# Row tiles of a group transposed and measured during two products instead of four, and two closing sums one product later

## The chip, the core and the metric

The kernel runs on one core of a Trainium2 chip. Its engines are TensorE (PE in the profile; PEld is its weight loads), VectorE (DVE), ScalarE (ACT), GpSimd (POOL) and SyncE (SP), which only issues DMAs here. Each engine works through its own instructions in order, and semaphores tie the engines together. The metric is the time of one execution in microseconds on the device, the median of several runs; less is better.

## The reference

Inputs are q, k, v of shape (8, 8, 576, 64), a threshold `tau`, and two matrices of 512 x 2048 and 2048 x 512. All is fp32.

```
scores = 0.125 * q @ k^T                       # per batch and head, 576 x 576
scores = where(scores >= max(row) - tau, scores, -1e9)
attn   = softmax(scores) @ v                   # (8, 8, 576, 64)
x      = attn with heads side by side          # (8, 576, 512)
u      = x + real(fft over 512 of fft over 576 of x)
un     = (u - mean(u)) / sqrt(var(u) + 1e-6)   # over the 512 columns
out    = u + relu(un @ w_ch1) @ w_ch2
```

## The kernel before, in words

**Three kinds of work are interleaved by hand.** The order of the program is the order of each engine's queue; nothing is reordered later.

*Attention.* For each batch there are four pairs of heads, and for each pair five row tiles of queries (four of 128 rows, and a short one made of the two heads' last 64). One pass of the main loop handles one row tile `i`: `scores` (L440, L446) puts the scores of two heads into PSUM; `softmax_first` takes row maxima on VectorE (L520) and exponentials on ScalarE (L526); `softmax_second` applies the threshold and sums on VectorE (L540, L385, L388); `softmax_third` scales on ScalarE (L549). The row tile before it is meanwhile transposed on TensorE (L587, L605: tiles `pe` and `pw`) and copied out by ScalarE (L593, L607). Twice per pair the product with v follows (L636).

*Mixing.* When a batch's attention is done, the two Fourier transforms are products with cosine and sine tables (`mixing`, L743: `py` at L766, `pa` at L783 and L787). Their PSUM tiles are copied out by ScalarE (L771, L776, L799) or summed by VectorE (L803, L804). The result, `u` transposed (`u_t`), has channels in the partitions and tokens along the free dimension. Sums over folded inputs (`fold_rows` L669 with L687 and L692, `partial_sums` L725, and L751 to L756) prepare it. `settle` (L459) lets a mixing overwrite `u_t` only when the groups before have read their rows.

*The two products with the big matrices.* Tokens are handled in nine groups of 512. The first group uses plain products (`channels`, L904). The other eight use `two_level` (L1107), which replaces ordinary block products with Winograd's seven-product form, applied twice. First comes the product with the first matrix: 28 quanta of matmuls (L1210). Then the product with the second matrix: seven **products** `m` in the order `L1 = (1, 2, 5, 4, 6, 7, 3)`, numbered `at = 0..6`, each of seven **quanta** `jn = 0..6` of four matmuls (L1398). Quanta 0 to 3 of a product fill one PSUM bank `po`, quanta 4 to 6 a second one. After quantum 3 and after quantum 6 the bank is copied out by ScalarE (L1410) or added to a running sum by VectorE (L1412, L1418). Jobs on other engines hang at certain quanta in the table `side` (`at_slots(at, slots, jobs)`): combinations of operands for the next product (`l2_forms`, L1191; `l1_form`, L1168), `gather` (L1274 to L1278, run by `plus`, L1263), and `finish`, which adds a finished quarter, times 1/std, to the rows (`Rows.add`: reciprocal L890 once per group, then L895).

The last group (`whole`, g = 8) has another form for its last products and another table of jobs.

**Row tiles.** The result needs `u` with tokens in the partitions. `Rows.load(t)` (L854) transposes the `t`-th 128 tokens: four transposes on TensorE into one PSUM tile `pn` (L858), then four copies by ScalarE into the tile `u` (L863, L864). It also leaves a job in `measures`: mean and variance on VectorE (`bn_stats` L869, `bn_aggr` L870). The main loop runs the waiting jobs with `measure()` right after `softmax_second`. When a group's four rows are loaded, `two_level` appends it to `wanted`; the main loop, after `softmax_third`, then calls `factors()` (L879): pending statistics first, then on ScalarE a square root (L881) and an exponential that brings back the exponential's table (L884), each with a table load. `finish` does the same itself where the main loop hasn't yet. In the first and in the last stretch of the kernel, statistics follow at once on the load.

**What sets the order.** In each pass the main loop calls `fill` three times: `fill(True)` between `softmax_first` and `softmax_second`, one between the two halves of the transposed weights, one after `softmax_third`. Each gets a budget of matmul columns (`per_slot`, about 3,900) and draws quanta (2048 columns each) from the group in work until it is spent; a row tile counts 512 columns, in a step of its own. While mixing goes on, a step of it is drawn first. Jobs hung at quanta within `fill(True)` are held back until after `softmax_second` and the statistics.

**Buffers.** All of `pe`, `pw`, `pv`, `pn`, `py`, `pa`, `ph` and `po` share four PSUM banks (tag "mm", `bufs=4`); the scores take the other four. The rows' tiles `u` have four buffers. The weights' blocks come from DRAM in loads of four quanta each into three buffers (`ensure`, L1068), issued two loads ahead.

The places that the change touches are the job table (L1341) and the end of each quantum (L1419 to L1426) in `two_level`:

Of the kernel before, what the change touches and what calls it, by code (L numbers as in the profile page):

```python
# [47 lines left out]
def kernel(  # L48
# [1038 lines left out]
    def block(g, second, index):  # L1087

        n = len(LOADS) * (g - 1) + (7 if second else 0) + index // PER
        if index % PER == 0:  # L1090
            ensure(n + 2 if g > 1 or second or index < 20 else n + 1)
        return w1[n % 3][:, 512 * (index % PER) : 512 * (index % PER + 1)]

    def quadrant(k, i):
# [7 lines left out]
    v_u, v_11, v_22, v_21, v_12 = (  # L1102
        w2_all[:, 3072 + NV * n : 3072 + NV * (n + 1)] for n in range(5)
    )
    v_22_21 = w2_all[:, 3072 + 2 * NV : 3072 + 4 * NV]

    def two_level(g, rows):  # L1107
# [157 lines left out]
        def twice(x):  # L1265
            return bass.AP(
                tensor=x.tensor, offset=x.offset, ap=[list(x.ap[0]), [0, 2], list(x.ap[-1])]
            )

        def gather(eng, v):  # L1270

            v = v.rearrange("p (j n) -> p j n", n=128)
            return [
                plus(eng, v[:, 1:5:3], twice(v[:, 0])),  # L1274
                plus(eng, v[:, 5], v[:, 4]),
                plus(eng, v[:, 6], v[:, 2]),
                plus(eng, v[:, 6], v[:, 4]),
                plus(eng, v[:, 2:4], twice(v[:, 5])),  # L1278
            ]
# [19 lines left out]
        def finish(i, n, v):  # L1299
            if wanted:  # L1300
                wanted.pop().factors()
            v = v.rearrange("p (j n) -> p j n", n=128)
            cols = slice(256 * n, 256 * n + 256)
            second = v[:, 3]
            second = bass.AP(
                tensor=second.tensor, offset=second.offset,
                ap=[list(second.ap[0]), [-128, 2], [1, 128]],
            )
            return [
                lambda: rows.add(2 * i, cols, v[:, 1:7:5]),  # L1310
                lambda: rows.add(2 * i + 1, cols, second),
            ]
# [8 lines left out]
        def at_slots(at, slots, jobs):  # L1321
            for jn, job in zip(slots, jobs, strict=True):
                side.setdefault((at, jn), []).append(job)

        whole = g == NG - 1
# [12 lines left out]
        at_slots(3, (0,), l1_form(s1_tile, s1_tile, a11, (V, V, V, V))[3:4])  # L1338
        at_slots(4, (1, 2, 4, 6), l1_form(a12, a12, s1_tile, (P, P, P, P)))
        at_slots(2, (0, 1, 2, 3, 4), gather(P, v_11))  # L1340
        at_slots(4, (2, 4), [lambda n=n: finish(0, 0, v_11)[n]() for n in range(2)])  # L1341
        if not whole:
            at_slots(
                5, (0,), [lambda: P.tensor_tensor(out=v_12, in0=v_u, in1=v_22, op=ALU.add)]
# [15 lines left out]
        def slot(at, jn):  # L1360
            while held:
                held.pop(0)()
            held.extend(side.get((at, jn), ()))
            while held and not holding:
                held.pop(0)()

        def plain_product(at, m):

            x = a[m].rearrange("p (k s i n) -> p k i s n", k=2, i=2, n=128)
            banks = plain[m] = [  # L1370
                ps.tile([128, 512], FP32, tag="mm", bufs=4, name="po")[:, 0:256] for _ in range(2)
            ]
            for jn, (n, k, at_) in enumerate(((0, 0, 0), (0, 1, 1), (1, 1, 2), (1, 0, 3))):
                right_ = plain_block(m, at_)
                for i in range(2):
                    for s in range(4):
                        nc.tensor.matmul(  # L1377
                            banks[i][:, 128 * n : 128 * n + 128], x[:, k, i][:, s],
                            right_[:, 128 * s : 128 * (s + 1)],
                            start=jn == 0 and s == 0, stop=jn % 2 == 1 and s == 3,  # L1380
                            skip_group_check=True,
                        )
                slot(at, jn)
                if at < 6 or jn < 3:
                    yield 4096

        for at, m in enumerate(L1):
            if whole and at > 4:
                yield from plain_product(at, m)
                continue  # L1390
            for jn, j in enumerate(J):
                if jn in (0, 4):
                    bank = ps.tile([128, 512], FP32, tag="mm", bufs=4, name="po")
                c0 = 128 * (jn % 4)
                to = bank[:, c0 : c0 + 128]
                right_ = block(g, True, 7 * at + jn)
                for s in range(4):
                    nc.tensor.matmul(  # L1398
                        to, lefts[m][j][:, s], right_[:, 128 * s : 128 * (s + 1)],
                        start=jn in (0, 4) and s == 0, stop=s == 3, skip_group_check=True,  # L1400
                    )
                if jn in (3, 6):
                    first, end = (0, 512) if jn == 3 else (512, NV)
                    src = bank[:, 0 : end - first]

                    def here(v):
                        return v[:, first:end]

                    if m in (1, 5, 4):
                        nc.scalar.copy(here({1: v_u, 5: v_22, 4: v_21}[m]), src)  # L1410
                    elif m == 2:
                        V.tensor_tensor(out=here(v_11), in0=here(v_u), in1=src, op=ALU.add)  # L1412
                    elif m == 6 and whole:
                        to = v_22_21.rearrange("p (two n) -> p two n", two=2)[:, :, first:end]
                        V.tensor_tensor(out=to, in0=to, in1=twice(src), op=ALU.add)
                    else:
                        to = here(v_12 if m == 3 else v_u)
                        V.tensor_tensor(out=to, in0=to, in1=src, op=ALU.add)  # L1418
                slot(at, jn)  # L1419
                if jn == 3 and at < 4:  # L1420
                    rows.load((2, 3, 0, 1)[at])
                    if at == 3:
                        wanted.append(rows)
                    yield ND * 128
                if jn < 6:
                    yield 2048  # L1426
            background()
            if m != 3:
                yield 2048
# [39 lines left out]
    def background():  # L1469

        if late:
            fold_more()
# [157 lines left out]
    def start_batch(b):  # L1630

        nonlocal groups, todo, per_slot, budget
        mixes.append(mixing(b))
        todo += MIX
        while groups < NG and BT * (groups + 1) <= (b + 1) * S:
            rows = Rows(groups)
            work.append((b, channels(rows) if groups == 0 else two_level(groups, rows), rows))
            todo += cost(groups)
            groups += 1

        keep = 4 * BT * (NJ - 2) * DM // 128 if b == 0 else 3 * 7 * 2048
        per_slot = (todo - spent - keep) / (3 * per_batch)
        budget = spent
# [103 lines left out]
    for i in range(2 * per_batch, total):  # L1747


        n, t = divmod(i, NT)  # L1750
# [157 lines left out]
```

## Time and profile before

| what | value |
|---|---|
| median of 3 runs | 1552.85 us (1552.24 to 1553.26) |
| the profiled execution | 1552.55 us |
| its span, first to last instruction | 1550.8 us |
| granted TensorE clock, mean | 0.999 |
| row tile's transposes (L858) | 144, 273 ns each by the profile |
| row tile's copies (L863, L864) | 72 and 72, 283 and 293 ns |
| statistics (L869, L870) | 36 and 36, 682 and 182 ns |
| closing sums of quarters (L895, 256 columns) | 64, 622 ns |
| table loads (L881, L884) | 9 and 9, 1283 ns |

The second-level products of groups 1 to 8 start at 441.0, 607.3, 778.1, 949.0, 1118.1, 1287.5, 1405.1 and 1499.7 us. In each of these groups the row tiles are now loaded after quantum 3 of products 0, 1, 2 and 3; in group 4 at 954.6, 966.3, 975.0 and 987.8 us. From about 1327 us on no attention is left, and the rest of the products and of the mixing runs alone.

How to read it: times are in microseconds unless marked ns. Matmul ends are modelled, and matmuls overlap, so the duration of a matmul says less than the distance between starts. In a row of the timeline, the first number is the start from the beginning of the span, the second the duration, and the bracket at the end the idle time of that engine just before, with what ended it. In a row of waits, "A <- B" means that A sat idle until B was done.

### The profile page before, as it was taken

How to read it: one execution, taken by the hardware profiler on the slowest of the kernel's cores; microseconds unless marked ns; L12 is line 12 of the kernel's file. 1: busy time of each engine (PE TensorE's matmuls, PEld its weight loads, DVE VectorE, ACT ScalarE, POOL GpSimd, SP SyncE). 2: the span in 40 equal slices, each digit the busy share in tenths (PEclk: the TensorE clock that was granted, in tenths of full speed). 3: DMA queues.
4: the chain of work that ended last, by engine and by line, in shares of the span. 5: the costliest groups of instructions: out<-in, count | busy, mean ns of one | idle time of the engine just before them, and what ended most of it. 6: DMA issues, size and time to landing. Idle time of an engine off the chain costs nothing.

```text
span 1550.8 us, 27036 instructions
## 1 busy us (share of the span) xinstructions
PE 1523.1 (98%) x9786; PEld 1185.1 (76%) x9786; DVE 1066.9 (69%) x2141; ACT 917.1 (59%) x1921; POOL 776.8 (50%) x964
## 2 busy tenths in 40 slices
PE   8999999999999999999999999999999999999999
PEld 5555555556788777877788778887788778989999
DVE  7987676846779466866588566956687666746546
ACT  6875675655656576656766666666666676232131
POOL 3775553034365643545254724555264626646635
PEclk9999999999999999999999999999999999999999
DMA  6423233465866344634464354635464534646655
GB/s 168 132 59 119 78 92 108 136 204 159 269 200 189 111 150 133 195 102 141 143 186 140 117 159 135 195 93 166 125 191 135 159 117 140 221 163 226 236 198 184
DMA packets 248907, 239.31 MB, mean 154 GB/s; under 512 B 197027, under 2 KB 218533, under 8 KB 228678
## 3 DMA queue, kind: packets, MB, share of 16 engines
q1 hardware_dynamic: 246262, 237.28, 50.1%
q8 instruction: 78, 1.28, 0.3%
q10 hardware_dynamic: 2512, 0.30, 0.1%
q14 instruction: 55, 0.45, 0.1%
HBM read 205.93 MB, written 31.46 MB: 153 GB/s over the span
## 4 chain that ended last, share of the span: by engine, by line
PE 84%; DVE 9%; ACT 3%; DMA 1%; POOL 1%; issue 1%; SPq 0%; ACTq 0%; DVEq 0%; POOLq 0%
PE ph L1210 25%; PE po L1398 18%; PE sc L440 9%; PE pv L636 9%; PE pw L605 7%; PE po L933 4%; PE ph L909 2%; PE sc L446 2%; PE py L766 2%; PE pa L783 1%; PE pe L587 1%; PE pa L787 1%; PE pm L360 1%; PE po L1377 1%; PE pn L858 1%
## 5 line engine op out<-in xcount | busy, mean ns | idle before, releaser
L520 DVE TENSOR_REDUCE neg<-sc 128x1 f32<-128x576 f32 x216 | 154.2, 750 | 113.0 <-PE sc L440 99.6
L526 ACT ACTIVATE e<-sc,neg 128x576 f32<-128x576 f32 x216 | 158.6, 734 | 121.6 <-DVE neg L520 121.5
L1147 DVE TENSOR_TENSOR hs<-ph,hs 128x512 f32<-128x512 f32 (+1 forms) x128 | 105.4, 823 | 168.0 <-PE ph L1210 97.7
L1398 PE MATMUL po<-w,w_all 128*128 128x128 f32 x1728 | 219.4, 276 | 0.3 <-ACT ends L593 0.3
L1398 PEld LDWEIGHTS po<-w,w_all 128*128 128x128 f32 x1728 | 205.0, 192 | 9.4 <-issue 4.0
L1156 POOL TENSOR_TENSOR w<-hs 128x512 f32<-128x512 f32 x32 | 42.1, 1317 | 313.8 <-ACT hs L1152 240.0
L540 DVE SCALAR_TENSOR_TENSOR e<-sc,thr,e 128x576 f32<-128x576 f32 x216 | 168.3, 812 | 20.6 <-ACT thr L530 20.6
L1210 PE MATMUL ph<-u_t,w 128*128 128x256 f32 x768 | 180.9, 382 | 0.5 <-DMA w<-f 0.5
L440 PE MATMUL sc<-kT,qT 64*128 64x288 f32 x1024 | 169.8, 431 | 7.1 <-DVE e L477 6.1
L607 ACT COPY e_t<-pw 128x512 f32<-128x512 f32 x256 | 148.6, 595 | 44.1 <-PE pw L605 42.7
L605 PE MATMUL pw<-ident,e 128*128 128x128 f32 x1152 | 168.8, 273 | 6.0 <-ACT ends L593 1.9
L549 ACT ACTIVATE e<-e,den 128x576 f32<-128x576 f32 x216 | 157.4, 775 | 8.9 <-DVE den L388 8.2
L1210 PEld LDWEIGHTS ph<-u_t,w 128*128 128x128 f32 x768 | 140.9, 190 | 23.6 <-issue 5.3
L1210 PE MATMUL ph<-w_all,w 128*128 128x256 f32 x672 | 157.1, 382 | 1.1 <-DVE w_all L1132 1.0
L605 PEld LDWEIGHTS pw<-ident,e 128*128 128x128 f32 x1152 | 134.8, 141 | 21.9 <-issue 5.6
L1152 ACT ACTIVATE hs<-hs 128x512 f32<-128x512 f32 (+1 forms) x96 | 74.1, 772 | 114.5 <-DVE hs L1147 113.7
L1210 PEld LDWEIGHTS ph<-w_all,w 128*128 128x128 f32 x672 | 123.4, 190 | 23.9 <-issue 4.9
L440 PEld LDWEIGHTS sc<-kT,qT 64*128 64x128 f32 x1024 | 96.3, 187 | 57.1 <-issue 23.7
L1263 POOL TENSOR_TENSOR w_all<-w_all 128x128 f32<-128x128 f32 (+2 forms) x160 | 118.4, 757 | 29.1 <-DVE w_all L1418 20.2
L1398 PE MATMUL po<-w,hs 128*128 128x128 f32 x912 | 120.0, 278 | 0.3 <-ACT ends L593 0.3
L1398 PEld LDWEIGHTS po<-w,hs 128*128 128x128 f32 x912 | 109.9, 192 | 9.9 <-issue 8.0
L593 ACT COPY ends<-pe 128x128 f32<-128x128 f32 (+1 forms) x128 | 38.1, 298 | 58.7 <-PE pe L587 40.1
(227 smaller groups left out, 2945.3 us busy)
## 6 DMA issues: line engine op xcount, KB each, us to landing
w<-f SPq DMA_DIRECT2D x150, 1024.0 KB, 4.9
hs<-in_moe_w_ch_dram SPq DMA_DIRECT2D x23, 512.0 KB, 4.7
q_in<-in_q_dram SPq DMA_DIRECT2D x128, 72.0 KB, 4.3
out_dram<-u SPq DMA_DIRECT2D x36, 256.0 KB, 2.5
k_in<-in_k_dram SPq DMA_DIRECT2D x124, 72.0 KB, 2.4
v_in<-in_v_dram SPq DMA_DIRECT2D x64, 128.0 KB, 5.0
f<-w SPq DMA_DIRECT2D x14, 512.0 KB, 3.3
f<-w SPq DMA_DIRECT2D x7, 1024.0 KB, 4.8
```

The costliest lines, as they stand in the source:

```text
L440: nc.tensor.matmul(sc[j][:, c, 0:HALF], qT[hp, 128 * t : 128 * t + 128], kT[hp, k0 + HALF * c : k0 + HALF * (c + 1)], start=True, stop=True,)
L520: nc.vector.tensor_reduce(out=neg[:, j : j + 1], in_=sc[j][:, :, 0:HALF], axis=AXIS_XY, op=ALU.max, negate=True,)
L526: nc.scalar.activation(out=ej, in_=sc[j][:, :, 0:HALF], func=ACT.Exp, bias=neg[:, j : j + 1], scale=1.0)
L540: nc.vector.scalar_tensor_tensor(out=ej, in0=sc[j][:, :, 0:HALF], scalar=thr[:, j : j + 1], in1=ej, op0=ALU.is_ge, op1=ALU.mult, accum_out ...
L549: nc.scalar.activation(out=e[:, S * j : S * (j + 1)], in_=e[:, S * j : S * (j + 1)], func=ACT.Copy, scale=den[:, j : j + 1],)
L605: nc.tensor.transpose(pw[:, c, :], e[:, c0 : c0 + 128], ident[:, :])
L607: nc.scalar.copy(e_t[:, 4 * j : 4 * j + 4, qs], pw[:, :, :])
L636: nc.tensor.matmul(pv[64 * j : 64 * j + 64, 0:m], vt[:, 2 * c + j, :], e_t[:, 4 * j + c, 0:m] if c < 4 else ends[:, 0, 0:m], start=(c == 0 ...
L1147: nc.vector.tensor_tensor(out=to, in0=bank, in1=to if other is None else other, op=ALU.add)
L1210: nc.tensor.matmul(bank[:, 256 * q : 256 * q + 256].rearrange("p (two n) -> p two n", two=2), left[:, 256 * c + 128 * q : 256 * c + 128 * ...
L1263: return lambda: eng.tensor_tensor(out=to, in0=to, in1=other, op=ALU.add)
L1398: nc.tensor.matmul(to, lefts[m][j][:, s], right_[:, 128 * s : 128 * (s + 1)], start=jn in (0, 4) and s == 0, stop=s == 3, skip_group_check ...
```

## The change

In `two_level`, row tiles are loaded after quanta 3 and 6 of products 0 and 1 (before: after quantum 3 of products 0 to 3), in the same order 2, 3, 0, 1. The group is appended to `wanted` with the last of them, after product 1's last quantum. In all groups but the last, the two closing sums of the first quarter (`finish(0, 0, v_11)`: rows 0 and 1, columns 0 to 255) hang at quanta 2 and 4 of product 5 instead of product 4. In the last group they stay where they are.

```diff
         at_slots(2, (0, 1, 2, 3, 4), gather(P, v_11))
-        at_slots(4, (2, 4), [lambda n=n: finish(0, 0, v_11)[n]() for n in range(2)])
+        at_slots(
+            4 if whole else 5, (2, 4), [lambda n=n: finish(0, 0, v_11)[n]() for n in range(2)]
+        )
...
                 slot(at, jn)
-                if jn == 3 and at < 4:
-                    rows.load((2, 3, 0, 1)[at])
-                    if at == 3:
+                if jn in (3, 6) and at < 2:
+                    rows.load((2, 3, 0, 1)[2 * at + jn // 6])
+                    if (at, jn) == (1, 6):
                         wanted.append(rows)
                     yield ND * 128
                 if jn < 6:
```

## The prediction

> **What bounds the kernel now.** I read the page's first part, then the time by stages, then the waits of TensorE, then single stretches of the timeline. The totals:
>
> ```profile
> PE 1523.1 (98%) x9786; PEld 1185.1 (76%) x9786; DVE 1066.9 (69%) x2141; ACT 917.1 (59%) x1921; POOL 776.8 (50%) x964
> ```
>
> TensorE is busy for 98%, and everything else has gaps. Here a rule has to be weighed. The Trainium skill (page "Perfetto Trace Analysis", section "Identifying the Most-Contended Engine") says that matmul busy time is no measure of headroom, since matmuls are pipelined, and that the weight loads' busy share is. By it 24% of the span, 366 us, would be open. So I took neither figure, but the time from the start of one block of matmuls to the start of the next, less what the same pair of blocks usually takes. That leaves 53 us in the whole span, 29 of them in the first 440 us, ahead of any second-level product, and 24 after it, of which 12 come in crumbs of up to 0.15 us. The change moves no matmul off TensorE. Its effect can be only in these stalls, and in new ones.
>
> The waits of TensorE name the stalls inside the second-level products:
>
> ```profile
> PE py L766 <- ACT y_e L776: 2.4, 5, 0.7
> PE pw L605 <- ACT ends L593: 1.9, 1, 1.9
> PE pw L605 <- ACT w_all L1410: 1.5, 1, 1.5
> PE pw L605 <- DVE w_all L1418: 1.1, 1, 1.1
> PEld po L1398 <- ACT ends L593: 1.0, 2, 0.5
> ```
>
> (Waiter, releaser, us in total, times, longest. The 1.9 is before 300 us, out of the change's reach.) All are one kind: the four "mm" banks of PSUM are taken, and TensorE waits until an eviction on ScalarE or VectorE frees one. The first row recurs in the fifth to sixth product of the groups. In group 4 (products from 949.0 to 1037.5 us) the timeline shows how it arises:
>
> ```profile
> 1000.95 0.17 DVE L388 RECIPROCAL den<-den 128x2 f32<-128x2 f32 x1
> 1001.03 0.16 DVE L890 RECIPROCAL rstd<-rstd 128x4 f32<-128x4 f32 x1
> 1001.22 0.95 DVE L895 SCALAR_TENSOR_TENSOR u<-w_all,rstd,u 128x256 f32<-128x256 f32 x1
> ...
> 1004.36 0.48 DVE L895 SCALAR_TENSOR_TENSOR u<-w_all,rstd,u 128x256 f32<-128x256 f32 x1
> ...
> 1005.22 1.42 DVE L520 TENSOR_REDUCE neg<-sc 128x1 f32<-128x576 f32 x2
> ...
> 1006.06 0.74 ACT L526 ACTIVATE e<-sc,neg 128x576 f32<-128x576 f32 x1 [1.28 <-DVE neg L520]
> ...
> 1008.19 0.52 PEld L766 LDWEIGHTS py<-dim_s,f 128*128 128x128 f32 x4 [0.91 <-ACT y_e L776]
> ```
>
> (Start, us, engine, line; in brackets idle time and what ended it.) The scores were ready at 1002.0, but VectorE reached their maxima only at 1005.22, because it runs in order and had the closing sums (L890, L895) and the mixing sums ahead of them. The exponentials wait for the maxima, the eviction of the first py waits behind the exponentials on ScalarE, and TensorE waits for that bank. The same chain stands in groups 3 and 5.
>
> **The change part by part.**
>
> 1. *Closing sums of the first quarter (L895, with L890) from product 4 to product 5 (counted from 0).* In seven groups two sums and one reciprocal leave the place shown: 0.16 + 0.95 + 0.48 = 1.6 us less on VectorE ahead of those maxima. TensorE there lacks 0.83 us by the start-to-start count (0.91 idle in the weight loads less the usual 0.08). 1.6 covers it, so it goes: groups 3, 4, 5 at 839.0, 1008.2, 1177.6, together **2.5 us**. Group 1 has 0.35 at 497.4 of the same kind. Group 2 has 1.22 at 666.0, where pw waits for L1418, which stands behind the same sums (1.1 us there). Together **1.6 us**. In the new place one sum and the reciprocal (0.6 us) stand in front of the next iteration's maxima; VectorE comes there 1.6 us earlier than now, so these are no later. The other falls into a held stretch, behind the softmax, where VectorE idles 3.1 us before L1418 at 1018.7. Cover gone, each would cost at most its own 0.6 us. What is late next: only the store of rows 0 and 1, which still waits for the second half's sums.
>
> 2. *Statistics and factors earlier.* Per group the same four L869 + L870 (0.68 + 0.18 us), so nothing is added, but two leave the stretch from product 2 to 3. In group 4 the one at 989.34 runs straight before 5 us of folding (L687, L692) that also delay the maxima:
>
> ```profile
> 989.34 0.69 DVE L869 BATCH_NORM_STATS2 stats<-u 128x6 f32<-128x512 f32 x1
> 990.07 0.18 DVE L870 BATCH_NORM_AGGREGATE mv<-stats 128x2 f32<-128x6 f32 x1
> 990.17 1.79 DVE L687 TENSOR_TENSOR half<-x 128x287 f32<-128x287 f32 x2
> ```
>
> That gives part 1 another 0.9 us of margin. The factors (two table loads, square root, warming exponential) move from about 993 to about 975 us in group 4. In group 2 they ran from 651.5 to 654.6, and the 0.46 us stall at 656.6 (eviction of pe on ScalarE) stands right behind: **0.5 us** off.
>
> 3. *Transposes and evictions earlier.* Each row tile is four transposes (0.45 us of TensorE) and four copies (L863, L864: 0.8 us of ScalarE together), as many as before. In group 3 the third tile sat between two product banks and pw waited for the fifth bank (1.52 us idle, 1.68 by starts, at 808.6); with that tile gone four banks suffice: **1.7 us** off. Against it: a tile counts 512 columns in the fills, so the products' quanta slip by at most one from the end of product 0 to the middle of product 3, and are back after it. By that count all middle groups come to what group 3 has now: the last quantum of product 2's first bank and the first of its second are issued just after the scores, and product 3's first bank has to wait for an eviction that stands behind the exponentials. TensorE reaches it some 12.45 us after the scores of the short row tile (967.67 in group 4). VectorE, with two statistics in that iteration instead of one, starts the next maxima at about +9.95 instead of 976.78 - 967.67 = +9.1; two exponentials with the threshold take until +12.3, the eviction (L1410, 0.59) until +12.85. That is **0.4 us lost** in each of groups 2 to 5, **1.6 us**; from below 0, from above 1.3 (L1191 took 1.57 us there and takes 0.68 elsewhere). Elsewhere there is room: in product 1 VectorE idles 1.6 us before the maxima at 968.84, and the second tile of a product meets banks freed 0.5 us or more before.
>
> The factors in the new place are the second weighing. Rows: 1.28 + 0.30 + 1.28 + 0.20 = 3.1 us in a row:
>
> ```profile
> 651.51 1.28 ACT L881 ACT_TABLE_LOAD   x1
> 652.80 0.30 ACT L881 ACTIVATE rstd<-mv,eps 128x4 f32<-128x4 f32 x1
> 653.11 1.28 ACT L884 ACT_TABLE_LOAD   x1
> 654.40 0.20 ACT L884 ACTIVATE warm<-eps 128x1 f32<-128x1 f32 x1
> 654.51 0.46 ACT L1410 COPY w_all<-po 128x384 f32<-128x384 f32 x1
> ```
>
> The Trainium skill (page "ScalarE: Activation LUTs", section "What ACT_TABLE_LOAD costs") says the same 1283 ns for a load but 2.66 us for every switch with its drain, 5.3 us for two, and that speaks against the change. Begun at 975.2, 3.1 us end at 978.3, before the maxima let the exponential start at 978.4: free. 5.3 us end at 980.5, 2.1 us later, and the stall in front of product 3 becomes 2.5 us in four groups, 10 us. The copy at 654.51 starts straight behind the last activation, so I take the row's 3.1.
>
> 4. *No queue is passed.* Loading a row tile and its statistics issue no DMA. The weights' loads on SyncE (w<-f, 4.9 us to land, issued two loads of four quanta ahead) slip with their quanta by at most one, some 0.9 us; q, k and v queued behind them are wanted iterations later. GpSimd's gather of v_11 stays in product 2, so the sums wait for it less than now. The tail (groups 7 and 8) has TensorE dense, with no stall between 1450 and 1547 us; fewer statistics there buy nothing.
>
> **The sum.** Off: 2.5 + 1.6 + 0.5 + 1.7 = 6.3 us. On: 1.6, plus 0.8 that I put for bank waits which a new order of evictions makes (the trace has four such singles of 0.4 to 1.7 in eight groups). Net -3.9 us, on the profiled execution's 1552.55 (span 1550.8 and 1.75 around it): 1548.65. The median of the runs is 0.3 higher, so **1549.0 us**.
>
> **The rivals.**
>
> *The stalls are only moved (within 0.2%).* For it: TensorE's whole loss in the products is 6.3 us, and with banks this scarce a wait removed at one place is met at the next: if half of the gain is met again, 1552.85 - 3.1 + 2.4 = 1552.1 us. Against it: 839, 1008 and 1178 repeat to 0.01 us, so one cause is at work, and it is the one taken away.
>
> *Slower: product 3's first bank.* The mechanism of part 3, in the iteration after the short row tile: factors, two statistics and the exponentials ahead of one eviction. It decides when the loss in each of the four groups is over (6.3 + 3.1) / 4 = 2.35 us; with the page's table cost it is 2.5, and with 0.8 us for the rest the time is 1552.85 - 6.3 + 10 + 0.8 = 1557.4 us. For it: VectorE has no gap over 0.4 us between 971 and 983 us. Against it: the 3.1 us row.
>
> *The loads free the mixing, which may not begin to overwrite before a group's rows are read.* They don't: in group 4 the last tile is read at 987.8, and the mixing first asks at 1020.9, 33 us later. This alone would be no change, 1552.85.
>
> **How the numbers follow.** 0.2% of the time is 3.1 us, about what this kernel's measurement can tell from no change. Forecast case 0.50 (its own range 1546.4 to 1549.7, all faster); stalls moved 0.32 and mixing 0.03, both within; slower by the bank 0.15. So faster 0.50, same 0.35, slower 0.15. The range 1546.2 to 1554.8 leaves out some 0.05 below and most of the slower case above.
>
> **What would show it.** Right: no wait of py on L776 of 0.7 us in groups 3 to 5; pairs of L858 blocks at quanta 3 and 6 of products 0 and 1; maxima in the iteration of the first py at about 1 us after their scores instead of 3.2; L881 some 18 us earlier in a group. Wrong: TensorE waiting at the first quantum of product 3 for L1410 by over 1 us, a table block over 3.1 us long, or pw waiting for u's copies (L864).

## The result and the profile after

| | median of the runs | profiled execution | its span |
|---|---|---|---|
| before | 1553.05 us (1552.24 to 1553.77, 4 runs) | 1552.55 us | 1550.8 us |
| after | 1545.76 us (1543.60 to 1547.94, 4 runs) | 1547.94 us | 1546.2 us |

The ratio is 0.996, with a 95% interval of 0.9947 to 0.9973: faster by 0.3 to 0.5%. 1549.0 us was forecast, with a range from 1546.2 to 1554.8: the direction is right and the size too small. The median lies just below the range; the ratio, applied to the 1552.85 us that the forecast started from, gives 1546.6, just inside. In the kernel after, lines behind the job table are two higher: L1398 is L1400, L1410 is L1412, L1418 is L1420.

The first part of the page of the kernel after:

```profile
PE 1524.0 (99%) x9786; PEld 1186.0 (77%) x9786; DVE 1063.2 (69%) x2141; ACT 916.4 (59%) x1921; POOL 779.4 (50%) x964
```

No engine has fewer instructions. What shrank is the span between the same 9786 matmuls, 4.6 us in this pair of executions. The waits of TensorE (PE) in the kernel after show where (us in total, times, longest):

```profile
PE pw L605 <- ACT ends L593: 1.9, 1, 1.9
...
PE py L766 <- ACT y_e L776: 0.9, 5, 0.2
...
PE pw L605 <- DVE w_all L1420: 0.2, 1, 0.2
```

The 1.9 is the wait before 300 us that was out of reach. Of the others, py waits 0.9 us in five places instead of 2.4, the wait for L1418 (now L1420) fell from 1.1 to 0.2, and the rows of pw for L1410 (1.5) and of po for L593 (1.0 in the row of the weight loads) are gone. No row is new.

In group 4 the iteration of the first py read so before (the timeline, cut; the maxima followed at 1005.22):

```profile
1000.65 1.36 PE L440 MATMUL sc<-kT,qT 64*128 64x288 f32 x8
...
1002.10 0.85 DVE L751 TENSOR_TENSOR f<-sums,f 128x304 f32<-128x304 f32 x2
...
1007.51 0.62 ACT L771 COPY y_e<-py 128x256 f32<-128x256 f32 x1
...
1008.19 0.71 PE L766 MATMUL py<-dim_s,f 128*128 128x128 f32 x4 [0.67 <-ACT y_e L776]
```

It now reads so:

```profile
997.51 1.24 PE L440 MATMUL sc<-kT,qT 64*128 64x288 f32 x8
...
999.19 1.14 DVE L1420 TENSOR_TENSOR w_all<-w_all,po 128x512 f32<-128x512 f32 x2
1000.25 1.41 DVE L520 TENSOR_REDUCE neg<-sc 128x1 f32<-128x576 f32 x2
...
1001.42 0.75 ACT L526 ACTIVATE e<-sc,neg 128x576 f32<-128x576 f32 x1
...
1003.75 0.62 ACT L771 COPY y_e<-py 128x256 f32<-128x256 f32 x1 [0.77 <-PE py L766]
...
1004.43 0.71 PE L766 MATMUL py<-dim_s,f 128*128 128x128 f32 x4 [0.17 <-ACT y_e L776]
```

The maxima come 1.50 us after the scores' end (998.75) instead of 3.2. And ahead of L771 ScalarE now sits idle for 0.77 us until the first py is there: it is no longer late, it waits for TensorE. By starts, TensorE still lacks 0.34 us at 1004.43. The copy-out of the first py (L771, then L776) can begin only when that py is done, and TensorE has less other work in between than the copy-out takes. An emptier queue does not remove that.

The iteration after the short row tile, where the prediction put its loss and its slower rival:

```profile
971.85 1.28 ACT L881 ACT_TABLE_LOAD   x1
971.98 1.24 PE L440 MATMUL sc<-kT,qT 64*128 64x288 f32 x8
...
973.03 0.93 DVE L1191 TENSOR_TENSOR w_all<-w_all,hs 128x512 f32<-128x512 f32 x1
...
973.88 1.41 DVE L520 TENSOR_REDUCE neg<-sc 128x1 f32<-128x576 f32 x2
...
974.74 0.20 ACT L884 ACTIVATE warm<-eps 128x1 f32<-128x1 f32 x1
974.85 0.73 ACT L526 ACTIVATE e<-sc,neg 128x576 f32<-128x576 f32 x1
...
976.28 0.58 ACT L1412 COPY w_all<-po 128x512 f32<-128x512 f32 x1
...
977.37 1.95 PE L1400 MATMUL po<-w,hs 128*128 128x128 f32 x16
```

The eviction (L1412) is through at 976.86, and product 3 takes the bank at 977.37, 0.5 us later, without a wait. The factors' block, from the first table load to the exponential of the softmax behind it, takes 974.85 - 971.85 = 3.0 us. It is the row's 3.1 that holds, and not the 5.3 that the Trainium skill's page "ScalarE: Activation LUTs" (section "What ACT_TABLE_LOAD costs") gives for two switches.

**Where the time came from**, by the distance from the start of one block of matmuls to the next, less the usual distance:

| stall of TensorE (us of the kernel before) | before | after |
|---|---|---|
| py, groups 3, 4, 5 (839, 1008, 1178) | 3 x 0.83 | 3 x 0.34 |
| py, group 1 (497) | 0.35 | 0.34 |
| pw, group 2 (666) | 1.22 | 0.38 |
| po behind the factors (656.6) | 0.46 | 0 |
| po, first quantum of group 3's second products (778.1) | 0.42 | 0 |
| pw, group 3 (808.6) | 1.68 | 0 |

That is 4.9 us, and no stall of over 0.25 us is new behind 440 us. From the scores of pass 40 of the main loop, counted from 0 (some 274 us from the start, ahead of any changed work), to the end the traces take 1276.89 us before, 1271.15 after, 5.7 less; the other 0.8 us is in crumbs below 0.2 us. This stretch is used below, since the start differs from one execution to the next for another reason (last section).

### The profile page after: what moved, and what is told of

It is laid out like the page before. It is cut to its first block, busy times and chain, and to the rows that moved or that the text cites. A ratio compares the mean times of both kernels' runs of the same rounds, so it can differ in the third digit from the quotient of the medians.

```text
span 1546.2 us, 27021 instructions
## 1 busy us (share of the span) xinstructions
PE 1524.0 (99%) x9786; PEld 1186.0 (77%) x9786; DVE 1063.2 (69%) x2141; ACT 916.4 (59%) x1921; POOL 779.4 (50%) x964
## 4 chain that ended last, share of the span: by engine, by line
PE 91%; DVE 4%; ACT 2%; POOL 1%; DMA 1%; issue 0%; ACTq 0%; DVEq 0%; POOLq 0%
PE ph L1210 25%; PE po L1400 21%; PE pv L636 10%; PE sc L440 10%; PE pw L605 7%; PE po L933 4%; PE ph L909 3%; PE sc L446 2%; PE py L766 2%; PE pe L587 1%; PE pa L783 1%; PE pn L858 1%; PE pa L787 1%; PE pm L360 1%; PE po L1379 1%; DVE neg L461 1%
## 5 line engine op out<-in xcount | busy, mean ns | idle before, releaser
L520 DVE TENSOR_REDUCE neg<-sc 128x1 f32<-128x576 f32 x216 | 154.3, 751 | 117.1 <-PE sc L440 105.5
L1147 DVE TENSOR_TENSOR hs<-ph,hs 128x512 f32<-128x512 f32 (+1 forms) x128 | 105.3, 823 | 167.1 <-PE ph L1210 97.3
L1400 PE MATMUL po<-w,w_all 128*128 128x128 f32 x1728 | 219.4, 276 | 0.0
L1400 PEld LDWEIGHTS po<-w,w_all 128*128 128x128 f32 x1728 | 205.4, 192 | 7.4 <-issue 4.0
L440 PE MATMUL sc<-kT,qT 64*128 64x288 f32 x1024 | 168.4, 430 | 5.9 <-DVE e L477 5.5
L1263 POOL TENSOR_TENSOR w_all<-w_all 128x128 f32<-128x128 f32 (+2 forms) x160 | 121.7, 777 | 44.5 <-DVE w_all L1420 23.4
L440 PEld LDWEIGHTS sc<-kT,qT 64*128 64x128 f32 x1024 | 95.1, 186 | 55.4 <-issue 22.9
L1400 PE MATMUL po<-w,hs 128*128 128x128 f32 x912 | 119.8, 278 | 0.0
L1400 PEld LDWEIGHTS po<-w,hs 128*128 128x128 f32 x912 | 109.8, 192 | 9.5 <-issue 8.0
L636 PE MATMUL pv<-e_t,v_in 128*64 128x320 f32 (+1 forms) x512 | 72.1, 423 | 1.5 <-ACT e_t L609 0.8
```

The lines of the kernel that those rows point to most:

```text
L440: nc.tensor.matmul(sc[j][:, c, 0:HALF], qT[hp, 128 * t : 128 * t + 128], kT[hp, k0 + HALF * c : k0 + HALF * (c + 1)], start=True, stop=True,)
L520: nc.vector.tensor_reduce(out=neg[:, j : j + 1], in_=sc[j][:, :, 0:HALF], axis=AXIS_XY, op=ALU.max, negate=True,)
L636: nc.tensor.matmul(pv[64 * j : 64 * j + 64, 0:m], vt[:, 2 * c + j, :], e_t[:, 4 * j + c, 0:m] if c < 4 else ends[:, 0, 0:m], start=(c == 0 ...
L1147: nc.vector.tensor_tensor(out=to, in0=bank, in1=to if other is None else other, op=ALU.add)
L1263: return lambda: eng.tensor_tensor(out=to, in0=to, in1=other, op=ALU.add)
L1400: nc.tensor.matmul(to, lefts[m][j][:, s], right_[:, 128 * s : 128 * (s + 1)], start=jn in (0, 4) and s == 0, stop=s == 3, skip_group_check ...
```

## The experiments

All kernels compute the whole reference. "Trace" is the time from the scores of pass 40 to the end, against 1276.89 us of the kernel before. Ratios are against the kernel before on the same chip (medians 1552.09, 1551.12 and 1551.21 us in the three sets).

**Theories.** *A*, the prediction's: the closing sums ahead of the maxima cause py's stalls, so moving the sums clears these, while the earlier row tiles clear the one at 808.6 and the factors' place the one at 656.6. *B*: the row tiles do all, and the sums nothing. *C*: the slower rival's mechanism is there and has only a small margin.

**The changed kernel again**, as the measure for the others:

> The changed kernel once more, beside the kernel before on the same chip. The two traces differ by 5.7 us from the second-level products of group 1 on, so if nothing else counts, the gain is 5 to 6 us (ratio 0.9963). If the 7.3 us between the medians of the first runs are real, the ratio is 0.9953, and 1.6 us come from a place that the two traces do not show.

1546.83 us, ratio 0.9961 (0.9948 to 0.9973), trace -5.9 us. So the medians' 7.3 us did not come again: here they are 5.3 us apart. The two traces of the changed kernel differ by 0.2 us in the stretch behind pass 40, which is how fine this measure is.

**Row tiles moved, sums left in product 4** (against the changed kernel):

```diff
-        at_slots(
-            4 if whole else 5, (2, 4), [lambda n=n: finish(0, 0, v_11)[n]() for n in range(2)]
-        )
+        at_slots(4, (2, 4), [lambda n=n: finish(0, 0, v_11)[n]() for n in range(2)])
```

> Row tiles moved, closing sums left in product 4. Theory 1 (the prediction's: VectorE's queue ahead of the maxima costs TensorE the wait for py): the py stalls of groups 3 to 5 stay at about 0.8 us each and the wait of pw in group 2 at over 1 us, so it gains only what the tiles and factors do, 2.5 to 3 us. Theory 2 (the tiles alone clear VectorE's backlog, since the statistics ahead of the folding go): py stalls fall to 0.3 us without the sums being moved, and it gains all of the changed kernel's 5 to 6 us.

1547.96 us, ratio 0.9972 (0.9962 to 0.9983), trace -4.5 us. By medians it can't be told from the changed kernel; by traces 1.2 to 1.4 us are missing. Its waits of TensorE:

```profile
PE pw L605 <- DVE w_all L1418: 1.2, 1, 1.2
PE py L766 <- ACT y_e L776: 1.2, 5, 0.5
```

**Sums moved, row tiles left** (against the changed kernel):

```diff
-                if jn in (3, 6) and at < 2:
-                    rows.load((2, 3, 0, 1)[2 * at + jn // 6])
-                    if (at, jn) == (1, 6):
+                if jn == 3 and at < 4:
+                    rows.load((2, 3, 0, 1)[at])
+                    if at == 3:
```

> Closing sums moved to product 5, row tiles as before. Theory 1: the py stalls of groups 3 to 5 fall from 0.83 to about 0.34 us and the wait of pw in group 2 by about 0.8 us; 2.3 us gained; the single waits at 808.6 (1.68 us), 656.6 (0.46) and 778.1 (0.42) stay. Theory 2: nothing is gained, within 1 us of the kernel before.

1548.89 us, ratio 0.9984 (0.9975 to 0.9993), trace -1.6 us.

```profile
PE pw L605 <- ACT w_all L1412: 1.5, 1, 1.5
...
PE py L766 <- ACT y_e L776: 0.9, 5, 0.2
...
PE po L1400 <- ACT ends L593: 0.5, 2, 0.3
```

In both kernels py's stalls in groups 3 to 5 are already down to 0.34 us. So A and B are each half right: either edit alone takes all that can be taken there, and the two don't add. What only the sums take is in group 2 (the 1.2 of L1418 stays without them; by starts 1.38). In group 1 they take back what the row tiles alone add (0.35 us before, 0.66 with the tiles alone, 0.34 with both). What only the row tiles take are the 1.5 of L1410 (here L1412) and the waits on L593. The moved sums cost something of their own when alone: the py wait of the next iteration rises from 0.19 to 0.39 us in groups 3 to 5.

The sums that left were 1.6 us of work, but with the sums alone moved the maxima come only 0.74 us sooner after their scores (2.47 us instead of 3.21). The pair of folds L751 ahead of them took 0.85 us before. It takes 1.58 with the sums alone moved, where it starts while GpSimd (POOL) runs:

```profile
997.35 1.27 POOL L1168 TENSOR_TENSOR hs<-hs,w 128x512 f32<-128x512 f32 x1
997.76 1.58 DVE L751 TENSOR_TENSOR f<-sums,f 128x304 f32<-128x304 f32 x2
```

and 3.01 with the row tiles alone moved, where it meets two GpSimd operations:

```profile
995.22 3.01 DVE L751 TENSOR_TENSOR f<-sums,f 128x304 f32<-128x304 f32 x2
```

So nearly half of what left VectorE's queue was lost again, because the folds now came while GpSimd worked (last section).

**The factors at their old place**, all else changed:

```diff
                     rows.load((2, 3, 0, 1)[2 * at + jn // 6])
-                    if (at, jn) == (1, 6):
-                        wanted.append(rows)
                     yield ND * 128
+                if (at, jn) == (3, 3):
+                    wanted.append(rows)
```

> The changed kernel, but the group's factors (table loads, square root, exponential) made after quantum 3 of product 3, as in the kernel before. If the factors' place matters, the 0.46 us wait for the eviction of pe in group 2 comes back, and perhaps its like in groups 3 to 5: 0.5 to 2 us slower than the changed kernel. If only the tiles and the sums matter, it equals the changed kernel within 0.3 us.

1545.59 us, ratio 0.9963 (0.995 to 0.9975), trace -5.2 us, against -5.7 and -5.9 of the changed kernel. One row of waits is back:

```profile
PE po L1400 <- ACT ends L593: 0.6, 2, 0.3
```

By starts these are 0.45 us at 658.8 and 0.44 at 779.2. So the factors' old place causes both, and the move is worth 0.6 to 0.8 us by the traces, too little for the medians to show. At 658.8 the factors stand on ScalarE straight ahead of the eviction. At 779.2 they have been over for 120 us, so how they act there is open. What the traces show is that VectorE's L1147 ahead of it starts 6.45 to 6.47 us after its pass's scores in all five kernels with the factors late, and 6.10 in all seven with them early, and that no releaser stands at its wait in either.

**The factors' table block twice** in the changed kernel, to find how far C's margin reaches:

```diff
             nc.scalar.activation(out=warm[:, :], in_=eps[:, :], func=ACT.Exp)
+            nc.scalar.activation(
+                out=self.rstd[:, :], in_=self.mv[:, :, 1], func=ACT.Sqrt, bias=eps[:, :], scale=1.0
+            )
+            nc.scalar.activation(out=warm[:, :], in_=eps[:, :], func=ACT.Exp)
```

> The changed kernel with the group's factors made twice in a row (four table loads instead of two, 6.2 us of ScalarE instead of 3.1). Theory 3 (the slower rival's mechanism: the exponentials behind the factors hold the eviction that product 3's first bank needs): in the changed trace the eviction (L1412) ends at 976.86 us and the bank is wanted at about 977.5, so 3.1 us more leave TensorE waiting some 2.4 us in groups 2 to 5, and it is 8 to 10 us slower than the changed kernel. Its opposite (ScalarE has room there): under 2 us slower.

1567.64 us, ratio 1.0105 (1.0092 to 1.0118), trace 20.3 us above the changed kernel. The waits (lines are four higher here), then the timeline of group 4:

```profile
PE po L1404 <- ACT w_all L1416: 12.8, 5, 2.7
...
PE po L937 <- ACT ends L593: 2.5, 1, 2.5
```

```profile
982.20 1.28 ACT L881 ACT_TABLE_LOAD   x1
...
988.33 0.72 ACT L526 ACTIVATE e<-sc,neg 128x576 f32<-128x576 f32 x1
...
989.77 0.58 ACT L1416 COPY w_all<-po 128x512 f32<-128x512 f32 x1
...
990.40 2.05 PE L1404 MATMUL po<-w,hs 128*128 128x128 f32 x16 [2.52 <-ACT w_all L1416]
```

Four loads take 988.33 - 982.20 = 6.1 us, twice the 3.0, and TensorE waits 2.52 us for precisely the bank that the slower rival named. So C's mechanism is real. 3.1 us more give a wait of 2.5, which fits the margin of 0.5 us read above. Of the loss, 12.8 us are this wait in five groups (2 to 6) and 2.5 an eviction in the first group, whose factors are doubled too; by starts they are 13.6 and 2.7. Another 1.6 and 1.7 us in groups 2 and 3 come from a halved clock behind the wait (last section). By starts that makes 19.6 of the 20.3.

**Row tiles early, but the statistics of two of them at their old places**, and the sums in product 4 (against the changed kernel, cut: left out are the sums' lines, the list `kept`, and in `load` the second argument, which takes the statistics' job in place of `measures`):

```diff
-                    rows.load((2, 3, 0, 1)[2 * at + jn // 6])
-                    if (at, jn) == (1, 6):
-                        wanted.append(rows)
+                    rows.load((2, 3, 0, 1)[2 * at + jn // 6], kept if at else None)
                     yield ND * 128
+                if at in (2, 3) and jn == 3:
+                    measures.append(kept.pop(0))
+                    if at == 3:
+                        wanted.append(rows)
```

> Row tiles transposed early, closing sums in product 4, but the statistics of the last two tiles, and the factors, made in products 2 and 3 as in the kernel before. If it is the statistics' leaving VectorE's queue ahead of the folding that shortened the wait for py when the tiles alone were moved, the stalls of groups 3 to 5 return to 0.8 us: 1.5 us slower than with all of the tiles' work moved, and 1 us more for the factors. If it is the transposes and their banks, they stay at 0.34 us.

1547.26 us, ratio 0.9976 (0.9968 to 0.9985), trace -3.3 us. By starts py stays at 0.34 to 0.35 us in groups 3 to 5, so it is not the statistics' leaving that clears it; that falls as an explanation of the run with tiles alone. The 0.45 and 0.42 us that the factors' late place causes are back, as the factors are late here.

Two more runs split what is left of the row tiles' edit: their instructions, and the 512 columns that each is counted at in the fills. **The count alone, and the tiles without their count** (both against the kernel before):

```diff
                 if jn == 3 and at < 4:
                     rows.load((2, 3, 0, 1)[at])
                     if at == 3:
                         wanted.append(rows)
+                if jn in (3, 6) and at < 2:
                     yield ND * 128
```

> The kernel before, with row tiles, statistics, factors and closing sums where they were; only the fills' account of a tile's 512 columns is made after quanta 3 and 6 of products 0 and 1, so that the quanta of products 1 to 3 slip as in the changed kernel. Theory Q (the slip of the quanta gives VectorE more time in its densest pass): the py stalls of groups 3 to 5 go from 0.83 to 0.34 us and the single wait at 808.6 goes, 2.5 to 3 us gained. Theory T (the tiles themselves, their banks and copies): py stalls stay at 0.83 us, within 1 us of the kernel before.

```diff
-                if jn == 3 and at < 4:
-                    rows.load((2, 3, 0, 1)[at])
-                    if at == 3:
+                if jn in (3, 6) and at < 2:
+                    rows.load((2, 3, 0, 1)[2 * at + jn // 6])
+                    if (at, jn) == (1, 6):
                         wanted.append(rows)
+                if jn == 3 and at < 4:
                     yield ND * 128
```

> The opposite: tiles, statistics and factors early, but their columns accounted for at the old places (after quantum 3 of products 0 to 3), so that the quanta stay where the kernel before has them; closing sums in product 4. Theory Q: the py stalls stay at 0.83 us and the wait in group 3 stays or changes; at most 1 us gained. Theory T: py stalls at 0.34 us, 3.5 to 4.5 us gained, as with the tiles moved in full.

The count alone: 1553.28 us, ratio 1.0015 (1.0006 to 1.0025), trace +2.3 us. The tiles without it: 1549.83 us, ratio 0.999 (0.998 to 1.0), trace -1.1 us. The waits of the count alone:

```profile
PE pw L605 <- ACT w_all L1410: 3.2, 4, 0.9
PE py L766 <- ACT y_e L776: 2.4, 5, 0.7
```

By starts, pw's wait is new in groups 2, 4 and 5 (1.09 us each) and is 0.58 instead of 1.68 in group 3. The prediction's reading of the quanta was right: the slip brings all middle groups to the state that group 3 was in, and it is the tile's leaving that makes the banks suffice. But py is cleared in all three groups by both together only: with the count alone it stays at 0.83 us in groups 3 to 5, with the tiles alone in groups 4 and 5 (group 3 falls to 0.34). The timeline of group 4 shows where they differ, in VectorE's lead before the iteration of py: the last operation of the softmax before (L388) against the start of the next scores (L440), then the maxima (L520). First row tiles with their count (sums in product 4), then without it, then the count alone:

```profile
994.33 0.17 DVE L388 RECIPROCAL den<-den 128x2 f32<-128x2 f32 x1
...
996.90 1.24 PE L440 MATMUL sc<-kT,qT 64*128 64x288 f32 x8
...
1000.50 1.41 DVE L520 TENSOR_REDUCE neg<-sc 128x1 f32<-128x576 f32 x2
```

```profile
995.42 1.41 PE L440 MATMUL sc<-kT,qT 64*128 64x288 f32 x8
...
995.77 0.17 DVE L388 RECIPROCAL den<-den 128x2 f32<-128x2 f32 x1
...
1000.03 1.42 DVE L520 TENSOR_REDUCE neg<-sc 128x1 f32<-128x576 f32 x2
```

```profile
1000.23 1.35 PE L440 MATMUL sc<-kT,qT 64*128 64x288 f32 x8
1000.52 0.17 DVE L388 RECIPROCAL den<-den 128x2 f32<-128x2 f32 x1
...
1004.79 1.41 DVE L520 TENSOR_REDUCE neg<-sc 128x1 f32<-128x576 f32 x2
```

With both, L388 starts 2.6 us ahead of the next scores; with one of them, 0.3 us behind their start, as in the kernel before. The maxima then come 2.4 us after the scores' end with both, and 3.2 us after it with one. The run with the sums alone reaches 2.5 by the other way (lead as before, but the sums out of the queue). So over the runs the stall of groups 1 and 3 to 5 is 0.83 us where the maxima come 3.2 us after the scores' end, 0.66 where they come 3.0 us after it (group 1 in the runs with row tiles early and the sums in product 4), and 0.34 where they come 2.6 us or less after it. Above the floor it follows the maxima one for one, and some 0.5 us sooner (an estimate from these points) reaches the floor. How tile and count together make the lead was not settled. Traced is that the count moves one quantum, 0.89 us, from the pass of the short tile into the next one, which is the shortest (6.38 us before, 7.27 after), and that the tile's leaving takes 0.45 us off the pass behind it (11.0 to 10.55). In group 3 of the tiles alone, which has the lead and the floor, both passes are so (7.82 and 10.55 us) without the count; no run takes the two apart.

**The sums one product later still**, all else changed:

```diff
-            4 if whole else 5, (2, 4), [lambda n=n: finish(0, 0, v_11)[n]() for n in range(2)]
+            4 if whole else 6, (2, 4), [lambda n=n: finish(0, 0, v_11)[n]() for n in range(2)]
```

> The changed kernel with the closing sums yet one product later, at quanta 2 and 4 of product 6. If what is left of the py stalls (0.34 us) came from the sums or from VectorE at all, it falls; if it is the eviction of the first py itself (ScalarE idles 0.77 us before it in the changed kernel), it stays at 0.34 us and the time is the changed kernel's within 0.5 us.

1547.4 us, ratio 0.9973 (0.9962 to 0.9984), trace -3.3 us, 2.5 us worse than the changed kernel, where at most 0.5 was expected. py and group 2 stay as in the changed kernel; new, by starts, are waits of ph in the next group's first product for GpSimd's differences (L1132), 0.35 us at 530.2, 699.2, 868.8, 1037.7 and 1206.5. That names most of the loss. In group 1 one of the sums (520.35 us) now stands straight ahead of VectorE's L803, for which GpSimd waits (5.57 us instead of 5.38) before it works its way to L1132.

**py's step ahead of the fill**, all else changed, to let its copy-out start sooner:

```diff
+        early = i % per_batch in (3, 4)
+        if mixes and early:
+            mix(1)
         fill(True)
...
-        if mixes:
+        if mixes and not early:
             mix(1)
```

> The changed kernel with the mixing's step that goes between the halves of the softmax put ahead of the held quanta instead of behind them, in the two iterations with py tiles: TensorE then has two quanta between the first py and the second. If the rest of the stall is the first py's eviction, the 0.34 us go in groups 1 and 3 to 5, and some of the 0.19 us of the next iteration: 1 to 2 us faster than the changed kernel. If banks are held too long by it, a wait of pe or pw takes its place and nothing is gained.

1548.62 us, ratio 0.9984 (0.9976 to 0.9993), trace -2.6 us. Against the changed kernel 1 to 2 us of gain were expected, and 3 us are lost. In groups 3 to 5 the first py's stall stays (0.35 us), but not for the reason found above. Its copy-out now stands behind the exponentials, without the idle time that it had in the changed kernel:

```profile
1001.53 0.74 ACT L526 ACTIVATE e<-sc,neg 128x576 f32<-128x576 f32 x1
...
1002.15 0.63 ACT L771 COPY y_e<-py 128x256 f32<-128x256 f32 x1
```

So this run does not test the floor, and that the floor is the copy-out's own time rests on ScalarE's 0.77 us of idle time in the changed kernel. In groups 1 and 2 the first py's stall rises to 0.82 and 0.85 us, and the next py meets an eviction too:

```profile
PE py L766 <- ACT y_o L771: 3.0, 4, 0.8
PE py L766 <- ACT y_e L776: 1.2, 4, 0.7
```

By starts the next iteration's wait is 0.92 us in four groups. No version here is faster than the changed kernel by more than the intervals.

## Why the prediction was right in its direction and too small

| step | predicted | by the trace |
|---|---|---|
| part 1: py, groups 3 to 5 | -2.5 | -1.5 |
| part 1: groups 1 and 2 | -1.6 | -0.85, all but 0.01 of it in group 2 |
| part 2: factors, 656.6 | -0.5 | -0.46 |
| not predicted: factors, 778.1 | 0 | -0.42 |
| part 3: pw, 808.6 | -1.7 | -1.68 |
| part 3: product 3's first bank | +1.6 | 0 |
| reserve for new bank waits | +0.8 | 0 |
| crumbs | 0 | -0.8 |
| sum | -3.9 | -5.7 |

**Part 1** took a stall as something that goes to zero once the delay ahead of it is covered. The sums' leaving did cover it, though by 0.74 us and not by the 1.6 that the prediction read as cover, since the folds behind them became longer. But a floor of 0.34 us stays, the first py's own copy-out, and group 1's 0.35 us had been nothing else from the start. The trace before had the clue: 0.35 in a group without the crowded queue. Part 1 was also wrong in holding the sums alone responsible: the row tiles' edit clears the same stalls without them.

**Part 2** was right on 656.6. It missed 778.1, which has the same wait on L593 and which it didn't connect with the factors; the run with the factors late brings both back, the second in a way that stays open. Its "0.9 us of margin" from the statistics was not what counted: the run with late statistics keeps the floor.

**Part 3** was right on 808.6 and on the slip of the quanta, which the run with the count alone shows. The step that failed is the size of the loss at product 3's first bank, 0.4 us in each of four groups. It set the maxima at +9.95 us after the short row tile's scores, and they came at 973.88 - 965.03 = +8.85: it had let a slow form of L1191 (1.57 us) stand, which took 0.93 here. That is 0.64 of the 1.1 us between; the rest is not broken down. In both traces this L1191 started while a GpSimd operation ran and ended 0.55 us after it; only the GpSimd operation ended sooner after the change (at 973.41, 0.38 us after L1191's start, instead of 1.02). The eviction comes 0.5 us ahead of the need where the prediction had it 0.4 behind, and the loss of 1.6 us is 0.

**The reserve** of 0.8 us met nothing, and the crumbs gave 0.8 us that no step had. Part 1's 1.75 us too much and the 1.25 missed in 778.1 and the crumbs nearly cancel, by luck; so the difference of 1.8 us is mainly the 2.4 us of the two losses that didn't come. The prediction also saw no stall between 1450 and 1547 us; there is one idle row of 0.50 us, a wait for a weights' load at 1451.26, and it is still there after the change (0.6), so its conclusion stands.

**The rivals.** That the stalls are only moved is refuted: no wait is new. The slower one has the right mechanism and place, and fails by 0.5 us of margin plus the table block's 3.0 us; a block twice as long gives 2.5 us per group and a slower kernel. The mixing's wait for the rows plays no part: the gain lies in the waits of the table above, and none of them is for the rows.

## What to carry to other kernels

Price a wait down to its floor and not to zero: see what the same wait costs where nothing stands ahead of it (here 0.34 of 0.83 us), and where two parts of an edit relieve the same wait, count it once. Work taken out of a queue is not gained in full when what follows it then runs longer (here 0.74 of 1.6 us): read the durations in the place where they will stand. A step moved in a hand-written order also moves what the order's budget counts for it: look at the step and its count apart. Here the count alone costs 2.3 us, while tile and count together gain 4.5. A margin is best measured by doubling what eats it: 3.1 us more on ScalarE turned a margin of 0.5 us into a wait of 2.5.

## What the runs showed of the hardware

**VectorE beside GpSimd.** In the twelve traces of this case the folds L751, L752 and L754 (two inputs of 128x304) run 384 times. The 141 of them that took over 0.7 us all started while a GpSimd operation ran, and ended 0.33 or 0.34 us after that operation did. The other 243 took under 0.5 us, and none of them started during one. So here such an operation, if it starts beside GpSimd, is through only after GpSimd's operation is. No run moves GpSimd's work by itself; this is read from the traces.

**The clock.** The runs of one kernel spread by up to 0.3% (1543.60 to 1547.94 us, with mean granted clocks of 1.000 and 0.997), and the traces show what goes with it ahead of 190 us, where no edit reaches: the granted clock of TensorE falls to one half for stretches of 3.4 us, none to three times in an execution. The time by stages (busy us and instructions of PE, PEld, DVE, ACT and POOL, then the granted clock as a share, the DMA share and GB/s), after:

```profile
50.00:100.00 50.00, 46.48 (x237) 27.48 (x235) 43.03 (x99) 41.22 (x90) 35.64 (x41) 0.97 0.43 110
100.00:150.00 50.00, 47.20 (x285) 30.80 (x286) 38.43 (x92) 32.09 (x76) 29.38 (x60) 0.97 0.32 98
150.00:200.00 50.00, 48.52 (x212) 26.77 (x209) 36.18 (x86) 32.81 (x76) 27.72 (x32) 0.97 0.23 61
```

and with the sums alone moved:

```profile
50.00:100.00 50.00, 46.29 (x241) 27.43 (x239) 44.95 (x102) 42.55 (x93) 37.06 (x44) 1.00 0.44 110
100.00:150.00 50.00, 47.16 (x292) 30.81 (x293) 40.22 (x96) 32.15 (x75) 30.96 (x62) 1.00 0.32 98
150.00:200.00 50.00, 48.74 (x212) 26.40 (x210) 37.28 (x87) 35.21 (x80) 26.74 (x30) 1.00 0.23 61
```

A stretch at half clock shows as 0.97 of 50 us. Leaving out the kernel with the table block twice, pass 40 starts at 270.4 to 272.0 us in the executions without one, at 272.3 to 273.9 with one, at 273.2 with two and at 275.0 to 276.1 with three. From none to three that is some 1.5 us for each, though executions with the same number differ by as much. It is the size of the steps that this change is made of. Differences of 1 us were therefore read from the stretch behind pass 40, and not from medians of four runs.

Some follow on a gap of TensorE, others don't. In all eleven executions of these kernels 2.2 us pass between two starts of matmuls at 81 to 83 us; in six of them a halved stretch begins within 1.3 us of it, in five none does. With the table block twice, TensorE waits 2.5 to 2.7 us in six places; in groups 2 and 3 the wait is followed by one, at 644.5 and 818.6 us, and not in the other four. The same sixteen matmuls that took 2.05 us in group 4 then read so:

```profile
644.16 3.50 PE L1404 MATMUL po<-w,hs 128*128 128x128 f32 x16 [2.52 <-ACT w_all L1416]
```

So a wait of over 2 us can cost more than itself. The Trainium skill (page "TensorE: Matmul & The Clock Gate", section "What's actually happening") has the half clock come after an idle window of some 3.4 us, counted in windows that run free of the kernel. The length of the stretches, 3.4 us, agrees; the gaps here were shorter, 2.2 us between two starts and 2.5 us of wait. Where a window lies against the gap could explain why only some are followed by one, but no run here tests it. The waits of at most 1.7 us in the second-level products, which the change took away, were followed by none.
